# First loads in order of use, x half turned by its load, and B's token sums on VectorE, in a two-block attention kernel on one Trainium2 core

## The chip, the cores and the metric

The kernel runs on one core of a Trainium2 chip. The time is device microseconds of one execution. A profile is one execution taken by the hardware profiler; the other times are of executions without it. Engines: PE is TensorE's matmul, PEld its weight load, DVE is VectorE, ACT ScalarE, POOL GpSimd, SP SyncE, which here issues most loads and stores.

## What is computed

Two blocks on inputs of 2048 tokens and 640 features, 32 heads of 20, results side by side in one output of 2048 x 1280, all bf16:

```python
def _A_ref(x, wqkv, wo):                     # sliding-window attention, window 256
    q, k, v = split_heads(x @ wqkv)
    scores = einsum("bhqd,bhkd->bhqk", q, k) * Dh ** -0.5
    p = softmax(where(0 <= i - j < 256, scores, -1e9))
    return merge_heads(einsum("bhqk,bhkd->bhqd", p, v)) @ wo

def _B_ref(x, wqkv, wo):                     # linear attention
    q, k, v = split_heads(x @ wqkv)
    pq, pk = phi(q), phi(k)                  # phi(t) = t + 1 where t > 0, else exp(t); + 1e-6
    kv = einsum("bhsd,bhse->bhde", pk, v)
    z = einsum("bhsd->bhd", pk)              # sums over the 2048 tokens
    num, den = einsum("bhqd,bhde->bhqe", pq, kv), einsum("bhqd,bhd->bhq", pq, z) + 1e-6
    return merge_heads(num / den) @ wo
```

## The kernel before

The 2048 tokens are worked in four tiles of 512. Every piece of work (a matmul or a group of them, an eviction, a load) is an operation that names its engine and what it depends on. A list written out in the kernel, SEQ, holds all 2089 of them as index x 8 + engine, and they are issued in that order, so it fixes the order of every engine's queue. Each engine runs its queue in order. Operations of A and B are mixed in it.

For block A and a tile: x arrives turned (features on partitions), by a transposing load on SP (`load_x`, L553). The first tile is the exception: four plain loads of 128 tokens each (`x0n`, L1209), which PE turns with an identity (L1242), five transposes each, and DVE evicts. q and k are products with 512 columns (`proj`, L577), v with 320 (`proj_v`, L638). Weights for q and k are first copied into another column order (`cq`, `ck`). Scores go to PSUM in small tiles of the array (`attn`, L708), ACT takes the exponential of 2048 columns at a time (76 times, L724), DVE multiplies the edges by a mask (L736), and PE multiplies by v (L764, "PV", four head groups in a tile). Head groups are written to DRAM and read back in another layout (`a_out`: `oc`, and `osum` with the row sums), a row of reciprocals is made by ACT from a logarithm, DVE multiplies (L860), and `finish_rows` makes 128 output rows (L798: ten matmuls in two halves, two evictions, one store).

For block B: phi(k) of a block of 128 tokens (`b_keys`, L913) stays as `pk` (four tiles in the buffers K0 to K3). `b_sums` (L938) multiplies it with x. `b_z` makes z: 32 matmuls of a column of ones with `pk`, four side by side (L974), so that each of four groups of 32 partitions holds one quarter of the sum; DVE splits it into a high and a low bf16 part (L986, L989) out of PSUM, ten matmuls turn it into a column (L995), and DVE spreads that into `Zc` (L1002). `b_kvwo` multiplies the sums with wv (L1037) and wo (L1055), evicts six rows of 120 (`kvs`), stores them to DRAM and reads them back as `kvwo`. `b_query` makes phi(q) (L1107; ACT L874, DVE L878 and L881), the denominators (`den`, 20 matmuls with 32-column weights, L1125), their reciprocals by ACT, four loads that spread them over the partitions (L1146), the division by DVE (L1171, one product for each 128 tokens), and the output rows (`finish_rows`, L798).

Output rows and `kvs` use four row buffers, O0 to O3: an eviction waits until the store of the row that had the buffer has landed. PSUM gives four banks (F0 to F3) to everything but scores. DVE sets the tile `warm` and a constant `tiny`, PE starts with 20 matmuls of 128 columns on `warm` and four pairs more (`heat`, L1185), and ACT loads its function table first and then issues three of the five loads of wv.

Of the kernel before, what the change touches and what calls it, by code (L numbers as in the profile page):

```python
# [7 lines left out]
P = 128  # L8
ALU = mybir.AluOpType
# [5 lines left out]
PRM = {"sq": "SP", "dens": 4}  # L15
TUNE = {}
SEQ = [
# [372 lines left out]
def build(nc, pools, A_x, A_wqkv, A_wo, B_x, B_wqkv, B_wo, out):  # L390
# [3 lines left out]
    HV = Dh + 1  # L394
    KT = 5
    NT = 16
    NQ = 512
    NTT = 4
    HALF = 320
    WIDE = bool(PRM.get("wide"))  # L400
    SWD = 640 if WIDE else 512
    scale = float(Dh) ** -0.5
    NF = 3 if WIDE else 4
    FB = [f"F{i}" for i in range(NF)]
    pl = Planner(FB + ["S0"] + [f"O{i}" for i in range(PRM.get("nosb", 4))] + ["L0"])

# [385 lines left out]
    def finish_rows(tb, col0, lhs, rhs, key, deps, name):  # L792
# [20 lines left out]
        if SEQ or PRM.get("ast"):  # L813
            st.engs["ACT"] = 430
# [668 lines left out]
```

## Time and profile before

| | us |
|---|---|
| median of 3 runs (lowest, highest) | 250.89 (250.74, 251.39) |
| the profiled execution | 250.49 |
| its span, first to last instruction | 248.8 |
| PE, ACT, DVE busy | 239.9, 200.8, 172.6 |

How to read it: in the chain of waits a piece is a start, a length and the work, followed back from the last instruction to what released it. "x16" counts instructions. In a timeline, brackets hold the idle time of the engine before the piece and what ended it. "F" and "S" are PSUM banks, F for all but scores. Line numbers are those of the kernel before. A few per cent of the matmuls have no record.

### The profile page before, as it was taken

The page shows a single profiled execution, that of the slowest core. Times are in us where ns is not written, and L with a number is a line of the kernel's source. Part 1 is how long each engine was busy: PE and PEld are TensorE (multiplying, and loading weights), DVE is VectorE, ACT ScalarE, POOL GpSimd, SP SyncE. Part 2 cuts the span into 40 slices and gives each one's busy share as a digit, 9 for nine tenths or more (in the row PEclk, how much of TensorE's full clock was granted, in tenths as well). Part 3 has the DMA queues.
Part 4 walks back from the last instruction along what each step waited for, and adds up shares of the span by engine and source line. Part 5 has one row for each costly group of instructions (what it writes and reads, how often), then busy time and mean ns, then how long its engine had stood idle before and what let it go on. Part 6 is the DMA issues. An engine that isn't in the chain of part 4 may idle for free.

```text
span 248.8 us, 9643 instructions
## 1 busy us (share of the span) xinstructions
PE 239.9 (96%) x4167; PEld 144.3 (58%) x4193; DVE 172.6 (69%) x441; ACT 200.8 (81%) x222; POOL 40.4 (16%) x93
## 2 busy tenths in 40 slices
PE   7999999999999999999999999999989999999993
PEld 6644565454655666545566666666555665565671
DVE  2553587778679978886666363369999899949740
ACT  2459898988999999988998788789999987946532
POOL 6003460063002601004078000000000000000000
PEclk9999999999999999999999999999999999999999
DMA  6999226649364759913573768863545472236433
GB/s 216 284 148 243 59 66 148 154 90 166 87 223 111 198 99 213 277 42 72 143 194 75 124 154 258 202 164 105 159 139 151 119 167 84 76 114 186 135 128 111
DMA packets 54216, 36.61 MB, mean 147 GB/s; under 512 B 34249, under 2 KB 52761, under 8 KB 54169
## 3 DMA queue, kind: packets, MB, share of 16 engines
q1 hardware_dynamic: 50537, 31.52, 49.7%
q0 software_dynamic: 2048, 2.63, 5.3%
q10 hardware_dynamic: 1584, 1.80, 2.2%
q8 instruction: 33, 0.54, 1.0%
q14 instruction: 14, 0.11, 0.2%
HBM read 13.90 MB, written 10.26 MB: 97 GB/s over the span
## 4 chain that ended last, share of the span: by engine, by line
PE 87%; ACT 6%; DVE 3%; issue 2%; DMA 1%; ACTq 0%; DVEq 0%
PE F L577 17%; PE F L798 16%; PE S L708 10%; PE F L638 9%; PE F L913 9%; PE F L938 9%; PE F L764 6%; PE F L1107 5%; ACT p L724 4%; DMA out_dram<-osb 1%; PE F L1185 1%; DVE pq L881 1%; PE F L1037 1%; ACT e L874 1%; PE F L1242 1%
## 5 line engine op out<-in xcount | busy, mean ns | idle before, releaser
L724 ACT ACTIVATE p<-S 128x2048 bf16<-128x2048 f32 x76 | 141.1, 1856 | 16.4 <-PE S L708 14.5
L736 DVE TENSOR_TENSOR p<-p,strip 128x256 bf16<-128x256 bf16 (+2 forms) x140 | 49.4, 381 | 21.1 <-ACT p L724 20.5
L874 ACT ACTIVATE e<-F 128x320 bf16<-128x320 f32 (+1 forms) x52 | 25.5, 501 | 8.3 <-PE F L1107 5.8
L638 PE MATMUL F<-wv,xT 128*128 128x320 bf16 x160 | 31.7, 300 | 0.1
L913 PE MATMUL F<-wkB,xT 128*128 128x320 bf16 x160 | 30.7, 299 | 0.2 <-issue 0.2
L798 PE MATMUL F<-woA,oc 128*128 128x320 bf16 x160 | 30.3, 300 | 0.0
L611 POOL DMA_DIRECT2D odd<-st x32 | 18.2, 573 | 69.3 <-ACT st L484 28.8
L577 PE MATMUL F<-xT,wk 128*128 128x512 bf16 x91 | 27.8, 380 | 0.3
L577 PE MATMUL F<-xT,wq 128*128 128x512 bf16 x92 | 26.9, 380 | 0.5 <-issue 0.3
L938 PE MATMUL F<-pk,xtok 128*128 128x320 bf16 x160 | 27.1, 300 | 0.0
L798 PE MATMUL F<-kvwo,pq 128*128 128x320 bf16 x160 | 25.9, 300 | 0.9 <-DVE pq L1171 0.4
L1107 PE MATMUL F<-xT,wqB 128*128 128x512 bf16 x91 | 25.4, 381 | 0.3
L486 DVE CAST ost<-F 128x512 bf16<-128x512 f32 x26 | 17.1, 685 | 10.2 <-PE F L764 10.0
L486 DVE CAST even<-F 128x512 bf16<-128x512 f32 x24 | 16.5, 688 | 8.2 <-PE F L577 7.9
L486 DVE CAST osb<-F 128x320 bf16<-128x320 f32 x33 | 15.5, 486 | 8.6 <-PE F L798 7.9
L608 POOL DMA_DIRECT2D odd<-even x32 | 16.6, 524 | 25.4 <-DVE even L486 23.2
L764 PE MATMUL F<-p,vt 64*32 64x320 bf16 (+4 forms) x720 | 20.5, 253 | 0.0
L638 PEld LDWEIGHTS <-xT 128*128 128x128 bf16 x160 | 15.1, 98 | 9.2 <-issue 1.3
L913 PEld LDWEIGHTS <-xT 128*128 128x128 bf16 x160 | 15.0, 98 | 8.9 <-issue 1.2
L764 PE MATMUL F<-p,sw 64*32 64x320 bf16 (+3 forms) x720 | 19.9, 253 | 0.2 <-DVE kvs L486 0.2
L798 PEld LDWEIGHTS <-pq 128*128 128x128 bf16 x160 | 14.9, 98 | 8.7 <-issue 1.6
L484 ACT CAST osb<-F 128x320 bf16<-128x320 f32 x31 | 12.6, 426 | 8.5 <-PE F L798 6.2
(85 smaller groups left out, 295.8 us busy)
## 6 DMA issues: line engine op xcount, KB each, us to landing
OD<-ost SPq DMA_DIRECT2D x32, 128.0 KB, 2.2
out_dram<-osb SPq DMA_DIRECT2D x24, 160.0 KB, 2.1
oc<-OD SPq DMA_DIRECT2D x4, 640.0 KB, 4.9
xtok<-in_B_x_dram SPq DMA_DIRECT2D x4, 640.0 KB, 4.5
odd<-even POOLq DMA_DIRECT2D x32, 48.0 KB, 2.9
sw<-vt SPq DMA_DIRECT2D x16, 87.0 KB, 3.1
out_dram<-osb ACTq DMA_DIRECT2D x8, 160.0 KB, 2.1
odd<-st POOLq DMA_DIRECT2D x32, 32.0 KB, 3.1
```

What stands on the lines that cost most here:

```text
L486: nc.vector.tensor_copy(out=dst, in_=src)
L577: nc.tensor.matmul(ps[:, a:b], lhsT=w[:, kt, i, :], rhs=xb["t"][:, kt, a:b], start=(kt == 0), stop=(kt == KT - 1))
L638: return lambda ps: nc.tensor.matmul(ps[:], lhsT=xb["t"][:, kt, bb * P : bb * P + P], rhs=rhs_(), start=(kt == 0), stop=(kt == KT - 1))
L708: nc.tensor.matmul(st["s"][64 * i : 64 * i + 64, o0 : o0 + b - a], lhsT=kb["t"][32 * j : 32 * j + Dh, sl, ko : ko + 64], rhs=qb["t"][32 * ...
L724: nc.scalar.activation(out=o_, in_=i_, func=ACT.Exp, scale=scale)
L736: nc.vector.tensor_tensor(out=x, in0=x, in1=mkv[:, None, :].to_broadcast([P, 4, 64 * w]), op=ALU.mult)
L764: nc.tensor.matmul(O[i][32 * j : 32 * j + 32, a:b], lhsT=lhsT, rhs=pb["t"][64 * i : 64 * i + 64, o0 + js * j : o0 + js * j + b - a], start ...
L798: return lambda ps: nc.tensor.matmul(ps[:], lhsT=lhs(c), rhs=rhs(c, hf), start=(c == 0), stop=(c == KT - 1))
L874: nc.scalar.activation(out=eb["t"][:, 0:n], in_=ps[:], func=ACT.Exp)
L913: return lambda ps: nc.tensor.matmul(ps[:], lhsT=xb["t"][:, kt, b * P : (b + 1) * P], rhs=R["wkB"][:, kt, hf * HALF : (hf + 1) * HALF], st ...
L938: return lambda ps: nc.tensor.matmul(ps[:], lhsT=R["xt", tb // 4][:, tb % 4, c * P : (c + 1) * P], rhs=R["pk", tb // 4][:, tb % 4, hf * HA ...
L1107: return lambda ps: nc.tensor.matmul(ps[:], lhsT=R["wqB"][:, kt, :].rearrange("p (f c) -> p c f", c=KT)[:, c, :], rhs=xb["t"][:, kt, :], s ...
```

## The change

- Loads: x's first block goes first on SP and its second first on ACT's queue (before, both on SP); wv follows on both. ACT's table load and its first activation become an operation (`tables`) that stands after ACT's first eviction.
- x's blocks 2 and 3 are turned by two transposing loads of 128 tokens on SP, in place of two plain loads, ten transposes and two evictions. The first tile of x has a block-wise layout, which its q, k and v matmuls read with a stride.
- Token sums: 15 adds on DVE accumulate the 16 blocks of `pk` in fp32 (`zacc`), then the high and low parts come from there in one piece each; the 32 matmuls at L974 go. `Zc` lies in the same buffer as the parts. Before the first denominator, 44 small matmuls are added (`dpad`).
- Warm-up: the operand is a constant of the program, not a tile that DVE sets; 18 matmuls and 16 small ones (`pad`), and two pairs instead of four.
- Row buffers: the buffers K2 and K3 hold output rows too, from when the high and the low part are made (until then a `hold` keeps them).
- PV: in the first tile the pieces are multiplied in their own order; in the others the order is as before.
- SEQ is written anew for the 2097 operations.

```diff
+PRM = {"sq": "SP", "dens": 4, "nwarm": 18, "pad": 4, "nfill": 2, "xT0": 2, "dpad": 11}
 SEQ = [
...
+    XT0 = PRM.get("xT0", 0)
...
+    XO = {"OK2": "K2", "OK3": "K3"} if PRM.get("xo", 1) else {}
+    pl = Planner(FB + ["S0"] + list(XO) + [f"O{i}" for i in range(PRM.get("nosb", 4))] + ["L0"])
+    held = [{} for _ in XO]
+    for g_ in held:
+        pl.op({"SP": 1}, lambda e: None, -(10 ** 8), [], name="hold", slots=(1, "O"), g=g_)
...
-        warm = mk("o", [P, NQ], BF16, "warm", tag="L0")
-        nc.vector.memset(warm[:], 0.0)
-        nc.scalar.preload_act_table_set("natural_log_exp_and_others")
+        warm = nc.const_aps.tensor(1.0, (P, P), BF16)
+        if not XT0:
+            nc.scalar.preload_act_table_set("natural_log_exp_and_others")
...
+                    rhs = xb["t"][:, :, kt, :] if t == 0 and XT0 else xb["t"][:, kt, a:b]
+                    nc.tensor.matmul(ps[:, a:b], lhsT=w[:, kt, i, :], rhs=rhs, start=(kt == 0), stop=(kt == KT - 1))
...
+                turn = [(x[2] - x[1], k, x, pb) for k, (lay, pb, _) in enumerate(ubox) for x in lay]
+                if t:
+                    todo = sorted(turn, key=lambda z: (-z[0], z[1]))
+                    turn = [y for k in range(len(todo) // 2) for y in (todo[k], todo[-1 - k])]
...
+    def row_tile(sb, name):
+        tag = sb["slot"][0]
+        return mk("over", [P, D], BF16, name, tag=XO[tag]) if tag in XO else mk("o", [P, D], BF16, name, tag="osb" + tag)
...
-        def emz(e):
-            ps = [psum(zg, hf, [P, HALF]) for hf in range(2)]
-            for b in range(4):
-                for hf in range(2):
-                    for s in range(4):
-                        nc.tensor.matmul(ps[hf][32 * s : 32 * s + 32, :], lhsT=ones[:], rhs=R["pk", s][:, b, hf * HALF : (hf + 1) * HALF], start=(b == 0), stop=(b == 3), tile_position=(0, 32 * s), skip_group_check=True)
...
+        for k in range(1, NT):
+
+            def add(e, k=k):
+                if "zacc" not in R:
+                    R["zacc"] = mk("const", [P, D], F32, "zacc")
+                blk = lambda i: R["pk", i // 4][:, i % 4, :]
+                nc.vector.tensor_tensor(out=R["zacc"][:], in0=blk(0) if k == 1 else R["zacc"][:], in1=blk(k), op=ALU.add)
+
+            need = pk_ops[2 * k : 2 * k + 2] + (pk_ops[0:2] if k == 1 else [prev])
+            prev = pl.op({"DVE": 730}, add, 4000 + k, need, name=f"zs{k}")
+            g_mm.append(prev)
+
+        def hi(e):
+            hl["t"] = mk("over", [P, 3, D], BF16, "hl", tag="T3")
+            nc.vector.tensor_copy(out=hl["t"][:, 0, :], in_=R["zacc"][:])
+
+        def lo(e):
+            nc.vector.tensor_tensor(out=hl["t"][:, 1, :], in0=R["zacc"][:], in1=hl["t"][:, 0, :], op=ALU.subtract)
+
+        hi_ = pl.op({"DVE": 730}, hi, EVK, [prev, gm], name="z.hi", rel=[(g_, 0) for g_ in held[0:1]])
+        evs = [hi_, pl.op({"DVE": 730}, lo, EVK, [hi_], name="z.lo", rel=[(g_, 0) for g_ in held[1:2]])]
...
+                for i in range(PRM.get("dpad", 0) if t == 0 else 0):
+                    for s_ in range(4):
+                        nc.tensor.matmul(dg["w"][32 * s_ : 32 * s_ + 32, 256:264], lhsT=ones[:], rhs=ones[:, 0:8], start=True, stop=True, tile_position=(0, 32 * s_), skip_group_check=True)
...
+            for i in range(pad):
+                for s_ in range(4):
+                    nc.tensor.matmul(psum(g)[32 * s_ : 32 * s_ + 32, 0:32], lhsT=warm[:, 0:32], rhs=warm[:, 0:32], start=True, stop=True, tile_position=(0, 32 * s_), skip_group_check=True)
...
+        for b, n in ((0, 1), (1, 1), (2, 2))[0 if XT0 == 1 else 2 :]:
+
+            def em(e, b=b, n=n):
+                for i in range(b, b + n):
+                    nc.sync.dma_start_transpose(out=x0_tile()[:, i, :, :], in_=xA[i * P : (i + 1) * P, :])
...
+        def tables(e):
+            nc.scalar.preload_act_table_set("natural_log_exp_and_others")
+            tinyo = mk("const", [P, 1], F32, "tinyo")
+            nc.scalar.activation(out=tinyo[:], in_=tiny[:], func=ACT.Exp)
...
+            x0l.append(dma(em, D_XROW, (-1000, -999, -994, -993)[b], [], name=f"x0n{b}", eng="ACTQ" if XT0 and b else "SP"))
```

More of the change, by code (lines that the diff above doesn't have):

```diff
@@ L637, in mm @@
                         rhs_ = lambda: wv[:, kt, :].rearrange("p (a i n) -> p a i n", a=2, i=2)[:, :, i, :]
+                        if t == 0 and XT0:
+                            return lambda ps: nc.tensor.matmul(ps[:], lhsT=xb["t"][:, bb, kt, :], rhs=rhs_(), start=(kt == 0), stop=(kt == KT - 1))
                         return lambda ps: nc.tensor.matmul(ps[:], lhsT=xb["t"][:, kt, bb * P : bb * P + P], rhs=rhs_(), start=(kt == 0), stop=(kt == KT - 1))
@@ L811, in finish_rows @@
             mms.append(g["mm"])
-        st = dma(lambda e: q_of(e).dma_start(out=out2[tb * P : (tb + 1) * P, col0 : col0 + D], in_=sb["t"][:]), D_STORE, -4000, ends, name="store")
-        if SEQ or PRM.get("ast"):
-            st.engs["ACT"] = 430
+        for a, b, need in [(0, 480, ends[:2]), (480, D, ends[2:])] if last else [(0, D, ends)]:
+            st = dma(lambda e, a=a, b=b: q_of(e).dma_start(out=out2[tb * P : (tb + 1) * P, col0 + a : col0 + b], in_=sb["t"][:, a:b]), (340, 1, int(420 * (b - a) / D), 350), -4000, need, name="store")
+            if SEQ or PRM.get("ast"):
+                st.engs["ACT"] = 430
+            R.setdefault("stores", []).append(st)
         st.rel = [(sb, 0)]
-        R.setdefault("stores", []).append(st)
         return mms
@@ L978, in b_z @@
         hl = {}
         evs = []
-        for hf in range(2):
-            cs = slice(hf * HALF, (hf + 1) * HALF)
-            def hi(e, hf=hf, cs=cs):
-                if "t" not in hl:
-                    hl["t"] = mk("over", [P, 2, D], BF16, "hl", tag="T3")
-                nc.vector.tensor_copy(out=hl["t"][:, 0, cs], in_=psum(zg, hf)[:])
-            def lo(e, hf=hf, cs=cs):
-                nc.vector.tensor_tensor(out=hl["t"][:, 1, cs], in0=psum(zg, hf)[:], in1=hl["t"][:, 0, cs], op=ALU.subtract)
-            a = pl.op({"DVE": dve_ps(HALF)}, hi, EVK, [zo, gm], name="z.hi")
-            evs.append(pl.op({"DVE": dve_ps(HALF)}, lo, EVK, [a], name="z.lo", rel=[(zg, hf)]))
+        prev = None
@@ L1058, in ev2 @@
                         if "t" not in sb:
-                            sb["t"] = mk("o", [P, D], BF16, "kvs", tag="osb" + sb["slot"][0])
+                            sb["t"] = row_tile(sb, "kvs")
                         copy(e, sb["t"][0:120, hf * HALF : (hf + 1) * HALF], ps[:])
@@ L1090, in em @@
             R["wqB"] = mk("w", [P, KT, D], BF16, "wqB", tag="wq")
-            nc.sync.dma_start(out=R["wqB"][:], in_=wBv[:, :, 0:D])
+            for a, b in WSP:
+                nc.sync.dma_start(out=R["wqB"][:, a:b, :], in_=wBv[:, a:b, 0:D])
         R["wq_op"] = dma(em, D_WFULL, key, [R["mm", "q", 3]], name="ld.wqB", earliest=140)
@@ L1184, in em @@
             for i in range(n):
-                nc.tensor.matmul(psum(g)[:, 0:P], lhsT=warm[:, 0:P], rhs=warm[:, 0:P], start=True, stop=True)
-        pl.op({"PE": n * 54}, em, key, [], slots=(1, "F"), g=g, rel=[(g, 0)], name="warm", ni=2 * n)
-    heat(nwarm, -(10 ** 8))
+                nc.tensor.matmul(psum(g)[:, 0:P], lhsT=warm, rhs=warm, start=True, stop=True)
+            for i in range(pad):
+                for s_ in range(4):
+                    nc.tensor.matmul(psum(g)[32 * s_ : 32 * s_ + 32, 0:32], lhsT=warm[:, 0:32], rhs=warm[:, 0:32], start=True, stop=True, tile_position=(0, 32 * s_), skip_group_check=True)
+        pl.op({"PE": n * 54 + pad * 14 + (95 if pad else 0)}, em, key, [], slots=(1, "F"), g=g, rel=[(g, 0)], name="warm", ni=2 * n + 8 * pad)
+    heat(nwarm, -(10 ** 8), PRM.get("pad", 0))
     for i in range(PRM.get("nfill", 4)):
         heat(2, 10 ** 7 + i)
-    pl.free["PE"] = 1450
+    pl.free["PE"] = 1060
     pl.free["SP"] = 1040
-    pl.free["ACTQ"] = 1500
-    pl.free["ACT"] = 2400
+    pl.free["ACTQ"] = 1040 if XT0 else 1500
+    pl.free["ACT"] = 3500 if XT0 else 2400
     pl.net = 2140
@@ L1237, in build @@
             W["c" + which].append(o)
-    for b in range(4):
+    for b in range((4, 0, 2)[XT0]):
         def tr(c, b=b):
@@ L1251, in build @@
         x0n_users.append(g["mm"])
+    x0["ready"] += x0.get("late", [])
     def em_wk(e):
         R["wkB"] = mk("w", [P, KT, D], BF16, "wkB", tag="wB")
-        nc.sync.dma_start(out=R["wkB"][:], in_=wBv[:, :, D : 2 * D])
+        for a, b in WSP:
+            nc.sync.dma_start(out=R["wkB"][:, a:b, :], in_=wBv[:, a:b, D : 2 * D])
     proj(0, "q", [-100, -99, -80, -79, -76], 1)
```

93 lines of the change are left out of this document (48 added, 45 removed), and 187 rows, old and new, of the table SEQ.

## The prediction

> **What bounds the kernel now.** I read the profile's page first, then the table of engine time by stretches, then the chain of waits with its pieces in order of time, and the timelines of single engines where that chain leaves TensorE.
>
> ```profile
> PE 239.9 (96%) x4167; PEld 144.3 (58%) x4193; DVE 172.6 (69%) x441; ACT 200.8 (81%) x222; POOL 40.4 (16%) x93
> ...
> PE 87%; ACT 6%; DVE 3%; issue 2%; DMA 1%; ACTq 0%; DVEq 0%
> ```
>
> TensorE (PE) is busy in 96% of the span and carries 87% of the chain. Work taken off it shortens the kernel one for one, unless ScalarE (ACT) or VectorE (DVE) is full in the same stretch. The stretches say where that is (columns: PE, PEld, DVE, ACT, POOL busy, clock, DMA share, GB/s).
>
> ```profile
> 0.00:10.00 10.00, 8.50 (x75) 7.13 (x76) 3.25 (x9) 2.40 (x5) 3.75 (x23) 1.00 0.78 238
> ...
> 140.00:150.00 10.00, 9.94 (x229) 6.70 (x214) 5.41 (x14) 8.27 (x7) 0.00 (x0) 1.00 0.49 115
> 150.00:160.00 10.00, 10.00 (x229) 6.48 (x228) 2.47 (x6) 7.88 (x7) 0.00 (x0) 1.00 0.94 249
> 160.00:170.00 10.00, 9.93 (x244) 6.26 (x243) 7.25 (x20) 8.38 (x9) 0.00 (x0) 1.00 0.59 157
> 170.00:180.00 10.00, 9.61 (x223) 6.07 (x223) 9.54 (x25) 9.73 (x11) 0.00 (x0) 1.00 0.47 144
> 180.00:190.00 10.00, 9.14 (x139) 5.35 (x140) 9.35 (x24) 9.78 (x12) 0.00 (x0) 1.00 0.46 129
> ...
> 220.00:230.00 10.00, 9.53 (x56) 5.73 (x56) 6.96 (x16) 5.15 (x11) 0.00 (x0) 1.00 0.60 176
> ```
>
> PE is idle 1.50 us in the first ten, 0.39 + 0.86 = 1.25 us between 170 and 190, where DVE and ACT are both nearly full, and 0.47 us between 220 and 230. DVE is half to three quarters free from 140 to 160. That is the map for what follows.
>
> The sum is made against the profiled execution: 250.49 us, of which the span is 248.8. The median of the runs is 250.89, 0.40 above it; I subtract from 250.49 and add the 0.40 at the end.
>
> **The start.** From the chain of waits:
>
> ```profile
> 1.17 0.27 DVE warm L504
> 1.44 0.04 DVE tiny L507
> ...
> 1.50 2.74 PE F L1185 x24
> 4.24 1.20 PE F L1242 x10
> ...
> 5.87 2.26 PE F L638 x16
> 8.13 0.28 PE F L1242 x5
> 8.41 0.27 PE F L638 x2
> 8.68 0.28 PE F L1242 x5
> 8.96 2.04 PE F L638 x15
> ```
>
> and from the timeline of the same stretch:
>
> ```profile
> 1.04 0.88 SPq L1209 DMA_DIRECT2D x0n<-in_A_x_dram  x2
> ...
> 4.70 2.74 SPq L542 DMA_DIRECT2D wkn<-in_A_wqkv_dram  x5
> 4.72 0.45 PEld L1242 LDWEIGHTS <-x0n 128*128 128x128 bf16 x5 [0.22 <-DMA x0n<-in_A_x_dram]
> ```
>
> The warm-up waits for two memsets of DVE until 1.50, while the load queue starts at 1.04. A constant that is there already takes this wait away: up to 0.46 us. The second row block of x then goes out first on ACT's queue instead of second on SP's, 0.88/2 = 0.44 us earlier, which covers the 0.22 us wait; wv's first loads on that queue are behind one issue of 0.44 us, but start 0.46 earlier. ACT's table load moves behind its first eviction, into time in which ACT is 24% busy. The 16 small matmuls (pad) fill time before x has landed. I take 0.40 of between 0 and 0.46: the first group of transposes followed the warm-up without a wait, so that x had landed. [...]
>
> Blocks 2 and 3 of x are turned by their load. That removes two groups of five transposes, 0.28 us each, on a PE that runs without a gap there: 0.56 us. What is late next is the turned load itself:
>
> ```profile
> xT<-in_A_x_dram SPq DMA_TRANSPOSE x3, 7.6
> ...
> x0n<-in_A_x_dram SPq DMA_DIRECT2D x4, 160.0 KB, 3.2
> ```
>
> ```profile
> L553 SPq DMA_TRANSPOSE xT<-in_B_x_dram x8: 2867/3020/4372, 14.4 to 199.0; - x8
> ```
>
> On SP it stands behind three plain issues, so from about 1.04 + 3 x 0.45 = 2.4. A turned load of 512 rows holds the queue 2.87 to 4.37 us; for 128 rows I estimate a quarter, 0.7 to 1.1, twice. Both are out by 4.6 us, where the weights wk, queued behind them, began before at 4.7, so those lose nothing. They land between 6.5 (second out at 3.3, the 3.2 of a plain load of that size) and 10.9 (the 7.6 of a load four times as large). PE wants them after the 20 v matmuls of blocks 0 and 1, 20 x 2.04/15 = 2.7 us after about 5.2, at 7.9. So a stall of 0 to 3.0 us; I take 0, as the plain load's row is the nearest in size, and keep the rest as a rival.
>
> **B's token sums.**
>
> ```profile
> 163.82 1.26 PE F L764 x92
> ...
> 165.88 0.42 PE S L708 x16
> 166.30 1.20 PE F L974 x32
> 167.50 0.34 PE F L1107
> ```
>
> ```profile
> L1002 DVE TENSOR_TENSOR Zc<-blk,zs x1: 826/826/826, 174.5 to 174.5; 128x640 bf16<-128x640 bf16 x1
> ...
> L986 DVE CAST hl<-F x2: 480/486/491, 167.6 to 168.0; 128x320 bf16<-128x320 f32 x2
> L989 DVE TENSOR_TENSOR hl<-F,hl x2: 481/482/484, 168.4 to 171.4; 128x320 bf16<-128x320 f32 x2
> ```
>
> The 32 matmuls at L974 are 1.20 us with PE work directly on both sides: gone in full, -1.20. In their place stand 15 adds on DVE of 128 x 640 and a high and a low part. The nearest row is the product with one fp32 operand over the same 640 elements, 0.83 us: 17 x 0.83 = 14.1, less the four old parts 4 x 0.48 = 1.9, so 12.2 us more on DVE. Its cover is the free time from 140 to 170, 4.6 + 7.5 + 2.75 = 14.8 us. The new order list, read as operations, puts six adds singly or in pairs between masks of A's third tile, seven in a row after the eviction of that tile's third head group, two behind its last masks, and the two parts among the fourth tile's first masks. Behind the seven wait masks whose exponentials ACT has yet to make. I charge nothing; if the cover is gone, each add is 0.83 us.
>
> **The padding before the first denominator.** 44 matmuls of 8 columns with 32-column weights are added on PE. The nearest row is an attention product (L764 above), whose 96 matmuls (92 of them recorded) also have 32-column weights in small tiles: 1.26/96 = 13 ns each, while it streams real columns as well: 44 x 13 ns = 0.58 us at most, 0 at least if PE waits there for its operands anyway. I take +0.30, halfway, because that row's streams hide part of its issue.
>
> **Row buffers and order.** Six buffers instead of four hold output rows, the two new ones only after the low part is made. Where four are too few, the chain shows it:
>
> ```profile
> 240.34 3.43 DMA out_dram<-osb
> ...
> 243.84 0.43 ACT osb L484
> ```
>
> and in the timelines, the first row that of the load queue:
>
> ```profile
> 180.78 4.56 SPq L1073 DMA_DIRECT2D kvd<-kvs  x4
> ...
> 244.32 0.84 PE L798 MATMUL F<-kvwo,pq 128*128 128x320 bf16 x5 [0.40 <-ACT osb L484]
> ```
>
> An eviction waits for a store to land, and the last five matmuls wait for that eviction. PE did other rows meanwhile, so what is won is not 3.43 but the 0.40 of idle PE. The same buffers take the kv rows, whose stores wait at 180.78 in the stretch where DVE and ACT are full; of the 1.25 us idle there I take 0.40, for most of it follows ACT's exponentials, which stay. Between 220 and 230:
>
> ```profile
> 224.75 0.69 DVE pq L881
> 225.44 0.41 DVE pq L1171
> 225.89 0.58 PE F L798 x3
> ```
>
> The rows of B's third tile wait for their division, which DVE does behind two feature maps. In the new list that division stands ahead of two of them and its reciprocals are spread first, so I take 0.40 of the 0.47. PV's pieces keep their number and columns: nothing.
>
> Sum: -0.40 - 0.56 - 1.20 + 0.30 - 0.40 - 0.40 - 0.40 = -3.06, so 247.4 for a profiled execution and 247.8 for the median.
>
> **The rivals.**
>
> *The turned load is late* (landing after 7.9): PE stands up to 3.0 us before the v products of block 3. For it speaks the 7.6 us of the large loads and a DMA share of 0.78 in the first ten us; against it a quarter of the size. Half of it gives 249.3, all of it 250.8; from 2.3 us on the result is no longer faster.
>
> *The clock comes late.* Ten transposes took 1.20 us from 4.24, of which 0.22 was a wait, so 98 ns each; five took 0.28 from 8.13, 56 ns each. The v matmuls from 5.87 run at 2.26/16 = 141 ns, near the later 2.04/15 = 136. So PE runs at about half rate for 5.87 - 1.50 = 4.4 us after its first matmul, although the granted clock of the row 0 to 10 is 1.00. The new warm-up is shorter, 18 x 2.74/24 = 2.1 us, and can leave PE idle before x lands. If that idle starts the 4.4 us anew at about 4.2, the work from 5.2 to 8.6 runs at half rate and 1.7 us are lost: 249.5. [...]
>
> *ScalarE takes the gain back.* From 170 to 190 ACT is 97 to 98% busy. If its exponentials set the time there, what was won before (0.96 + 1.20) and the 0.40 of the kv rows only lengthen that stretch's idle PE; what stays is 0.30 - 0.40 - 0.40 = -0.5, and the result is 250.4. Against it: ACT is only 79 to 84% busy from 140 to 170, so its exponentials can come earlier too.
>
> *VectorE delays the attention* and the kernel becomes slower. The queue is in order: if the seven adds in a row, 7 x 0.83 = 5.8 us, come when masks are ready, the product of that group waits, TensorE runs out of other groups because its banks wait for the same DVE, and ACT waits for free probability buffers. All of it on the path gives 247.8 + 5.8 = 253.6; it eats the gain from 3.1 us on and shows as slower from 3.9. For it speaks that four more additions stand just before the 9.54 of 170 to 180; against it the 2.47 of 150 to 160.
>
> **How the numbers follow.** About 0.3%, 0.75 us, is what a measurement of this kernel tells from no change: faster is under 250.14, slower over 251.64. The forecast has 0.60; late load 0.09, late clock 0.09, ScalarE 0.08, VectorE 0.14. Faster: 0.60 + 0.09 of the clock + 0.06 of the load + 0.02 of ScalarE, where it takes back only a part, = 0.77; within 0.3%: 0.03 + 0.06 = 0.09; slower: 0.14. The forecast's own range goes from 246.4 (all of the 1.25, 0.47 and 0.46 us, no padding cost, and the 0.13 us of idle PE from 140 to 170) to 248.9 (nothing at the start and at the kv rows, 0.28 more for the padding). The range for 8 in 10 reaches up over late clock, half of the late load and ScalarE's case to 250.6 and leaves out VectorE's case, the rest of the load's and a little below.
>
> **What would show it.** Right: warm-up from about 1.1 us, v matmuls from about 5.2 and no transposes after them; no matmul at the sums' line and adds of 0.75 to 0.83 us between 130 and 166; no wait for a store before the last matmuls; fewer than 0.2 us of idle PE after the third tile's reciprocals. Wrong: v matmuls over 0.2 us apart or waiting for xT between 7 and 11; PE idle before the attention product that stood at 163.82, with DVE on the adds; more than 1.25 us of idle PE between 168 and 190.

## The result: slower, and the profile after

The changed kernel took 254.6 us (median of 6 runs, 253.56 to 255.43), the kernel before, measured beside it, 251.14 (250.22 to 251.92): ratio 1.0137, 95% interval 1.011 to 1.0163. The profiled execution took 253.56 us with a span of 252.1 (before 250.49 and 248.8). It is one of the six and the fastest of them, so the two profiles differ by 3.07 us where the medians differ by 3.46. I had forecast 247.8 and a range up to 250.6.

The page of the changed kernel, engine busy times and the chain's shares:

```profile
PE 239.8 (95%) x4180; PEld 143.8 (57%) x4205; DVE 184.9 (73%) x452; ACT 202.1 (80%) x222; POOL 40.5 (16%) x92
...
PE 85%; DVE 5%; ACT 4%; issue 2%; DMA 2%; ACTq 0%; DVEq 0%
```

TensorE is busy as long as before, in a span that is 3.3 us longer, so the loss is time in which it stands. The stretches of the changed kernel:

```profile
0.00:10.00 10.00, 8.15 (x72) 6.09 (x73) 1.47 (x5) 4.17 (x6) 3.72 (x22) 1.00 0.86 235
...
150.00:160.00 10.00, 10.00 (x228) 6.33 (x227) 9.63 (x19) 8.20 (x8) 0.00 (x0) 1.00 0.79 186
160.00:170.00 10.00, 9.95 (x217) 6.20 (x217) 9.02 (x21) 9.62 (x11) 0.00 (x0) 1.00 0.43 135
170.00:180.00 10.00, 9.43 (x225) 6.37 (x225) 9.90 (x24) 9.74 (x10) 0.00 (x0) 1.00 0.58 155
180.00:190.00 10.00, 9.52 (x182) 5.86 (x182) 9.66 (x26) 9.40 (x10) 0.00 (x0) 1.00 0.66 125
190.00:200.00 10.00, 8.47 (x197) 5.27 (x197) 8.82 (x22) 8.95 (x8) 0.00 (x0) 1.00 0.60 143
...
220.00:230.00 10.00, 9.33 (x114) 5.49 (x96) 6.07 (x14) 4.72 (x11) 0.00 (x0) 1.00 0.51 146
```

and the one row of the kernel before that is not shown with the prediction:

```profile
190.00:200.00 10.00, 9.95 (x212) 6.03 (x219) 8.74 (x22) 9.79 (x10) 0.00 (x0) 1.00 0.50 141
```

Where VectorE got its adds, from 150 to 170, TensorE does not stand (0.05 us). It stands 1.53 us from 190 to 200, where it stood 0.05 before; 0.67 from 220 to 230 (0.47 before); and 1.85 in the first ten (1.50 before).

**The start.** Chain of waits, then timelines of TensorE and ScalarE:

```profile
1.97 4.54 DMA wv<-in_A_wqkv_dram
...
6.55 5.03 PE F L646 x32
```

```profile
1.08 2.08 PE L1207 MATMUL F<-const-bfloat16-1.0 128*128 128x128 bf16 x18 [1.08 <-PEq L1516]
3.09 0.30 PE L1210 MATMUL F<-const-bfloat16-1.0 128*32 128x32 bf16 x16
3.93 1.25 PE L1291 MATMUL F<-ident,x0n 128*128 128x128 bf16 x10 [0.54 <-POOL vt L541]
4.97 0.42 PE L1207 MATMUL F<-const-bfloat16-1.0 128*128 128x128 bf16 x2
5.42 0.72 PE L646 MATMUL F<-wv,xT 128*128 128x320 bf16 x2
5.93 0.42 PE L1207 MATMUL F<-const-bfloat16-1.0 128*128 128x128 bf16 x2
6.55 5.03 PE L646 MATMUL F<-wv,xT 128*128 128x320 bf16 x32 [0.20 <-DMA wv<-in_A_wqkv_dram]
```

```profile
2.94 1.28 ACT L491 ACT_TABLE_LOAD   x1 [2.94 <-issue]
4.68 0.69 ACT L491 COPY xT<-F 128x640 bf16<-128x640 bf16 x1 [0.46 <-PE F L1291]
5.39 1.28 ACT L1247 ACT_TABLE_LOAD   x1
```

The warm-up begins at 1.08 as forecast, but is over at 3.2, and x's first block lands at 3.88 (3.35 before). The v matmuls stop after two and go on at 6.55. In the trace each of the first ones holds TensorE for 267 ns, twice the 136 of later ones, until 7.57. The first scores begin at 18.55, 0.44 us later than in the profile before. ScalarE loads a table twice, once at its first copy (L491) and once where the program asks for it (L1247); before, there was one load.

**The stop at 198.** The tile `kvwo` (the transfer and who waited for it), and the load queue ahead of it:

```profile
L1099 SPq DMA_DIRECT2D kvwo<-kvd x2: 485/492/498, 189.0 to 195.0; - x2
...
  PEld L813: 1.6, 1
```

```profile
190.85 0.59 SPq L1088 DMA_DIRECT2D kvd<-kvs  x1
191.49 0.55 SPq L1168 DMA_DIRECT2D recB<-recS  x1
195.04 0.48 SPq L1099 DMA_DIRECT2D kvwo<-kvd  x1
```

The last store of B's small matrix goes out at 190.85, its read-back only at 195.04, and TensorE's rows wait for that until 199.59. The page's waits name a feature map on VectorE beside it (`pq` L897, done at 199.57); it is not the cause, for in run pe24 below the same rows begin at 198.61 and that feature map ends at 199.72. The new order list itself sends the store out 1.9 us later than the old one did (188.95).

**The end.** The last piece of the chain in the kernel before, then the chain of the changed kernel:

```profile
245.20 0.42 ACT osb L484
```

```profile
238.01 8.54 PE F L813 x62
...
246.57 0.49 DVE osb L493
```

The transfers after 245 us by queue (packets, MB, share), first of the changed kernel, then of the one before; q1 has what SP issues, q10 what ScalarE issues, q8 instructions:

```profile
q10 hardware_dynamic: 304, 0.34, 9.0%
q1 hardware_dynamic: 144, 0.16, 4.2%
q8 instruction: 1, 0.02, 0.9%
```

```profile
q1 hardware_dynamic: 288, 0.33, 8.6%
q10 hardware_dynamic: 144, 0.16, 4.2%
```

The last evictions no longer wait for a store: 62 matmuls without a break. But from the last eviction's end, 247.06, to the end of the span there are 5.02 us, where before there were 3.19. What is new there is one transfer on q8: 16 KB of instructions that begin at 246.95, after the last matmul, and take 1.52 us. Of the 432 packets of the last three stores 405 are done by 248.6; the other 27, a sixteenth, come one by one from the end of the fetch on, until 250.1.

### The profile page after: what moved, and what is told of

The parts are those of the page before. It is cut to its first block, busy times and chain, and to the rows that moved or that the text cites. A ratio compares the mean times of both kernels' runs of the same rounds, so it can differ in the third digit from the quotient of the medians.

```text
span 252.1 us, 9681 instructions
## 1 busy us (share of the span) xinstructions
PE 239.8 (95%) x4180; PEld 143.8 (57%) x4205; DVE 184.9 (73%) x452; ACT 202.1 (80%) x222; POOL 40.5 (16%) x92
## 4 chain that ended last, share of the span: by engine, by line
PE 85%; DVE 5%; ACT 4%; issue 2%; DMA 2%; ACTq 0%; DVEq 0%
PE F L813 18%; PE F L584 16%; PE S L717 10%; PE F L954 9%; PE F L929 9%; PE F L774 7%; PE F L647 7%; PE F L1123 6%; ACT p L733 2%; PE F L646 2%; DMA wv<-in_A_wqkv_dram 2%; DVE pq L897 1%; ACT e L890 1%; DVE p L745 1%; PE F L1146 1%
## 5 line engine op out<-in xcount | busy, mean ns | idle before, releaser
L954 PE MATMUL F<-pk,xtok 128*128 128x320 bf16 x160 | 28.3, 300 | 0.0
L584 PE MATMUL F<-xT,wq 128*128 128x512 bf16 x96 | 27.5, 380 | 0.3 <-issue 0.2
L584 PE MATMUL F<-xT,wk 128*128 128x512 bf16 x88 | 26.6, 380 | 0.5 <-ACT e L890 0.2
L647 PE MATMUL F<-wv,xT 128*128 128x320 bf16 x120 | 26.4, 300 | 0.1
L493 DVE CAST even<-F 128x512 bf16<-128x512 f32 x27 | 18.3, 688 | 7.7 <-PE F L584 7.3
L894 DVE TENSOR_SCALAR e<-e 128x320 bf16<-128x320 bf16 (+1 forms) x52 | 13.4, 260 | 9.8 <-ACT e L890 9.1
L774 PE MATMUL F<-p,vt 64*32 64x320 bf16 (+3 forms) x720 | 20.3, 253 | 0.0
L929 PEld LDWEIGHTS <-xT 128*128 128x128 bf16 x160 | 15.1, 98 | 8.9 <-issue 1.5
L491 ACT CAST osb<-F 128x320 bf16<-128x320 f32 x32 | 13.4, 425 | 7.7 <-PE F L813 7.6
```

The lines of the kernel that those rows point to most:

```text
L493: nc.vector.tensor_copy(out=dst, in_=src)
L584: nc.tensor.matmul(ps[:, a:b], lhsT=w[:, kt, i, :], rhs=rhs, start=(kt == 0), stop=(kt == KT - 1))
L647: return lambda ps: nc.tensor.matmul(ps[:], lhsT=xb["t"][:, kt, bb * P : bb * P + P], rhs=rhs_(), start=(kt == 0), stop=(kt == KT - 1))
L774: nc.tensor.matmul(O[i][32 * j : 32 * j + 32, a:b], lhsT=lhsT, rhs=pb["t"][64 * i : 64 * i + 64, o0 + js * j : o0 + js * j + b - a], start ...
L929: return lambda ps: nc.tensor.matmul(ps[:], lhsT=xb["t"][:, kt, b * P : (b + 1) * P], rhs=R["wkB"][:, kt, hf * HALF : (hf + 1) * HALF], st ...
L954: return lambda ps: nc.tensor.matmul(ps[:], lhsT=R["xt", tb // 4][:, tb % 4, c * P : (c + 1) * P], rhs=R["pk", tb // 4][:, tb % 4, hf * HA ...
```

## The experiments

All of them, with the time, that of the kernel before beside it, the ratio with its interval, and from the profiled execution the begin of the first scores and the time from the last eviction to the end of the span (18.11 and 3.19 in the kernel before):

| run | us | before | ratio (95%) | first scores | end |
|---|---|---|---|---|---|
| changed | 254.6 | 251.1 | 1.0137 (1.011, 1.0163) | 18.55 | 5.02 |
| pe24 | 251.67 | 250.8 | 1.0026 (1.0006, 1.0046) | 18.40 | 3.40 |
| kvq | 253.65 | 250.8 | 1.0109 (1.0084, 1.0133) | 18.83 | 5.44 |
| x0plain | 253.87 | 250.8 | 1.0113 (1.0085, 1.0141) | 21.82 | 5.29 |
| zpe | 254.85 | 250.8 | 1.0145 (1.0116, 1.0174) | 18.99 | 5.19 |
| before12 | 252.91 | 251.05 | 1.0058 (1.0036, 1.008) | 18.22 | 5.31 |
| warm26 | 250.77 | 251.05 | 0.997 (0.9945, 0.9995) | 18.66 | 3.37 |
| oldstart | 250.6 | 251.05 | 0.9963 (0.9938, 0.9988) | 18.33 | 3.25 |
| best1 | 250.86 | 251.05 | 0.9988 (0.996, 1.0017) | 17.75 | 3.37 |
| vorder | 249.49 | 250.96 | 0.9942 (0.9923, 0.9962) | 17.64 | 3.37 |
| vorder0 | 251.12 | 250.96 | 1.0003 (0.9985, 1.0021) | 17.58 | 4.59 |
| oldden2 | 250.7 | 250.96 | 0.9996 (0.9979, 1.0014) | 18.54 | 3.22 |
| rows | 250.74 | 250.96 | 0.9995 (0.9973, 1.0017) | 19.04 | 3.53 |
| padmove | 253.67 | 251.1 | 1.0106 (1.0053, 1.016) | 18.17 | 5.38 |
| vkvq | 250.17 | 251.1 | 0.9965 (0.9939, 0.9992) | 17.42 | 3.37 |

The first scores scatter from profile to profile: 18.11 to 19.04 with the old first loads, 18.17 to 18.99 and once 21.82 with the new ones, 17.42 to 18.66 with the new ones and a longer warm-up. A few tenths in that column of a single profile decide nothing.

### The end: pe24, before12

pe24:

```diff
-PRM = {... "dpad": 11}
+PRM = {... "dpad": 8}
```

> The changed kernel with 8 instead of 11 groups of the padding before the first denominator: TensorE's program is 24 instructions shorter, as long as that of the kernel before. Theory A (the 16 KB of TensorE's instructions that are fetched after the last matmul stand in front of the last stores): that fetch goes, the time from the last eviction to the end of the span falls from 5.0 us to 3.2-3.5, and the time from 254.6 to about 253.0. Rival (the last stores are slow because two queues issue them at once): the end stays 5.0 us long and the time falls by at most 0.1 us, for the 12 matmuls.

251.67 us: 12 matmuls of 8 columns fewer, and the ratio goes from 1.0137 to 1.0026, which is 2.8 us, more than the 1.6 expected. The 16 KB after 245 are gone from the transfers, and the end is 3.40 us long:

```profile
q10 hardware_dynamic: 294, 0.33, 8.8%
q1 hardware_dynamic: 144, 0.16, 4.2%
```

The surplus is the stop at 198. It shrank too, to 0.24 us of idle TensorE from 190 to 200, and all behind it came 1.0 us earlier than in the changed kernel:

```profile
190.00:200.00 10.00, 9.76 (x213) 5.85 (x203) 9.22 (x23) 8.61 (x9) 0.00 (x0) 1.00 0.50 133
```

Without these losses the change is still no gain: pe24 is 0.3% above the kernel before.

before12, the same length put into the kernel before, ahead of its first denominator:

```diff
                 ps = psum(dg, 0, [P, P])
+                for i in range(3 if t == 0 else 0):
+                    for s_ in range(4):
+                        nc.tensor.matmul(ps[32 * s_ : 32 * s_ + 32, 0:8], lhsT=ones[:], rhs=ones[:, 0:8], start=True, stop=True, tile_position=(0, 32 * s_), skip_group_check=True)
```

> The kernel before with 12 matmuls of 8 columns added ahead of its first denominator, 24 instructions with their weight loads, so that TensorE's program is as long as that of the changed kernel; they take 12 x 13 ns = 0.16 us. Theory A (behind a certain length of TensorE's program another 16 KB of it are fetched after the last matmul and stand in front of the last stores): a fetch of 16 KB appears after 244, the time from the last eviction to the end grows from 3.2 us to 4.5 or more, the time is 252.2 or more (before 250.8). Rival (that fetch, if it comes, hurts only the new order of the last rows): the time is within 0.4 us of 250.8.

252.91 us. The fetch after 245 appears, and the end grows from 3.19 to 5.31:

```profile
q1 hardware_dynamic: 288, 0.33, 8.9%
q10 hardware_dynamic: 182, 0.19, 4.9%
q8 instruction: 1, 0.02, 1.1%
```

So 0.16 us of work in a kernel with another order of its last rows costs 1.5 us by the ratio, 1.9 by the medians. In all profiles with the long program the end takes 5.0 to 5.4 us, in all with the short one 3.2 to 3.5 (one exception, vorder0, below). The theory holds, the rival falls. Why the fetch comes no run isolates. The queue q8 has 33 such fetches in the profile before and 34 in the changed kernel's, on average some 250 recorded TensorE instructions apart (8360 over 33, 8385 over 34). What pe24 and before12 show is that 24 TensorE instructions fewer take the one after the last matmul away and 24 more bring it. In the changed kernel TensorE's last matmul ends at 246.55, 0.4 us before the fetch begins, so TensorE does not wait for it; what is late beside it are the 27 packets that land from its end on.

### The stop at 198: kvq, padmove

kvq, order list only: the last product of B's small matrix (`kvwo2.1`) ahead of `oa2.1.1`, its eviction and store ahead of the first read-back, the second read-back (`kvr0`) behind the second of the loads that spread reciprocals.

> The changed kernel, only the order list edited: the last product of B's small matrix with wo, its eviction and its store go ahead of the third row block's second half, and the second read-back of the result ahead of two of the loads that spread reciprocals. Theory A (the 1.5 us that TensorE stands at 198 is the late read-back of that matrix): idle TensorE from 190 to 200 falls from 1.53 us to under 0.4, the rows at 199.6 begin at 198.2, the time is about 253.2. Rival (VectorE, filled by the adds, is what is late there): TensorE then waits for the division of pq instead, 0.9 us or more stay idle, and the time is above 254.0.

253.65 us. The read-back goes out at 192.13, idle TensorE from 190 to 200 is 0.17 us, but part of the gain is given back before, at 186, where the moved product makes everything 0.45 us later; the last matmul ends 0.34 us earlier than in the changed kernel, 0.62 if one takes off the later start of this run. The stop is the late read-back, as theory A has it; the time lies between the two forecasts, and its interval overlaps that of the changed kernel.

padmove, the padding before the second denominator instead of the first:

```diff
-                for i in range(PRM.get("dpad", 0) if t == 0 else 0):
+                for i in range(PRM.get("dpad", 0) if t == 1 else 0):
```

> The changed kernel with all 44 padding matmuls ahead of the second denominator instead of the first: the same program length, but from 186 to 204 us TensorE stands 88 instructions earlier in it, so that the fetch of 16 KB that began at 192.22 begins 3 us or more later. Theory A (that fetch shares an engine with the store of B's small matrix, which then lands after 4.2 us instead of 2.1 to 2.5, and the read-back and the rows behind it are late by as much): the second read-back is issued by 193.6 instead of 195.04, idle TensorE from 190 to 200 is under 0.5 us instead of 1.53, the end after the last eviction stays at 5 us, the time is 253.1 to 253.6 (changed kernel 254.6). Rival (the stop at 198 comes from the order of the queues alone, and run pe24 lost it by chance of its start): the stop stays above 1.0 us and the time is 254.2 or more.

253.67 us (251.94 to 254.66). In the profiled execution (252.2), TensorE does not stand at all from 190 to 200, while the end stays 5.38 us long. How long the store took to land, of the changed kernel, of pe24 and of padmove (KB, median us to landing):

```profile
kvd<-kvs SPq DMA_DIRECT2D x1, 100.0 KB, 4.2
```

```profile
kvd<-kvs SPq DMA_DIRECT2D x1, 100.0 KB, 2.5
```

```profile
kvd<-kvs SPq DMA_DIRECT2D x1, 100.0 KB, 2.5
```

The changed kernel's store went out at 190.85 and the fetch of 16 KB began at 192.22, 1.4 us behind it; in pe24 2.3 us behind (190.94, 193.28), in padmove 2.7 (190.22, 192.93). The fetch came later as expected, though by 0.7 us and not by 3. Where it meets the store, the landing and the read-back are late by 1.6 us. The other profiles fit: in the three in which a fetch begins within 1.4 us behind this store (the changed kernel, x0plain at 0.9, zpe at 0.5) it takes 4.2, 3.8 and 3.5 us to land, in the other thirteen, the kernel before among them, 2.0 to 3.2. That a late landing is the usual case of the changed kernel and not only that of the profiled runs stays open: padmove's six runs fall into two groups, 252 to 253 and 254.3 to 254.7.

### Token sums: zpe

```diff
-            prev = pl.op({"DVE": 730}, add, 4000 + k, need, name=f"zs{k}")
+        zo = pl.op({"PE": 1120}, emz, kv("z", key), [pk_ops, gm], mode="z", slots=(2, "F"), g=zg, name="z", cls="Z", ni=64)
```

and the high and low parts by halves out of PSUM, as in the kernel before.

> The changed kernel with the token sums again by 32 matmuls on TensorE and the four parts out of PSUM, in the place where the fourth tile's first masks stand; the 15 adds on VectorE go. Theory A (the adds lie in free time of VectorE and cost nothing): 1.2 us more on TensorE at about 167, everything behind it is later by that, the stop at 198 stays, the time is 255.5 to 255.9. Rival (the adds delay VectorE and so the rows from 170 on): the stop at 198 shrinks by 1 us or more and the time is 254.6 or less.

254.85 us, outside both forecasts and between them; four executions, and their interval overlaps that of the changed kernel. Against the changed kernel, whose order it has, the trace shows the scores that follow the sums 1.62 us later and the next ones 2.0. At the stop 1.4 us come back, since the read-back lands while TensorE is still behind. The last matmul ends 1.94 later, 1.50 without the later start. That is more than the medians show, which differ by 0.25 us: this profile is the slowest of four executions, that of the changed kernel the fastest of six. The 64 instructions more also move the fetch to 0.5 us behind the store, so zpe does not isolate the sums. TensorE, idle for 0.05 us from 150 to 170, does not wait for the adds where they stand:

```profile
L993 DVE TENSOR_TENSOR zacc<-zacc,pk x14: 817/824/827, 148.2 to 165.4; 128x640 f32<-128x640 f32 x14
...
L1001 DVE CAST hl<-zacc x1: 486/486/486, 168.3 to 168.3; 128x640 bf16<-128x640 f32 x1
L1004 DVE TENSOR_TENSOR hl<-zacc,hl x1: 817/817/817, 170.4 to 170.4; 128x640 bf16<-128x640 f32 x1
```

### The start: x0plain, warm26, oldstart

x0plain:

```diff
-                    nc.sync.dma_start_transpose(out=x0_tile()[:, i, :, :], in_=xA[i * P : (i + 1) * P, :])
+                    nc.sync.dma_start(out=x0_tile()[:, i, :, :], in_=xA[i * P : (i + 1) * P, :].rearrange("p (k n) -> p k n", k=KT))
```

> The changed kernel with the two turning loads of x's first tile replaced by plain loads of the same bytes to the same place, so half of that tile is not turned (the rest is computed as before). Theory A (the turning loads share the 16 DMA engines with wv's loads and hold wv back): wv is there by 5.7, the v matmuls run on from 5.4 without the stop until 6.55, the first scores come about 1.0 us earlier (17.6 instead of 18.6), the time is about 253.5. Rival (the second table load and the eviction of x's first block by ScalarE make the start late): v still stops until 6.5 and the time stays within 0.3 us of 254.6.

253.87 us; the time is near the theory's, with an interval that overlaps that of the changed kernel, but in the profile the theory falls: v stopped until 7.49. Of the 16 parts in which wv's third slice lands, 15 were there by 6.35, the last at 7.44; in the changed kernel 15 by 6.15 and the last at 6.51. So wv is late without turning loads too. This execution, with 256.74 the longest of its kernel, shows another cause:

```profile
7.49 5.76 PE L646 MATMUL F<-wv,xT 128*128 128x320 bf16 x21 [1.11 <-DMA wv<-in_A_wqkv_dram]
```

5.76/21 = 274 ns a matmul: TensorE went on at half rate until 13.3 us, and the first scores came 3.3 us later than in the changed kernel.

warm26 (with the short program):

```diff
-PRM = {..., "nwarm": 18, "pad": 4, "nfill": 2, "xT0": 2, "dpad": 11}
+PRM = {..., "nwarm": 26, "pad": 0, "nfill": 2, "xT0": 2, "dpad": 8}
```

> The changed kernel with the short program of run pe24 and a warm-up of 26 matmuls of 128 columns without the 16 small ones, so that TensorE is busy from 1.1 to about 3.9, when x's first blocks land. Theory B (the idle 0.7 us between warm-up and transposes makes the clock come late: v at 267 ns for 320 columns until 7.5 to 8.4 us, and to 13.3 in one run): v runs at 136 ns from 5.8 at the latest, the first scores come at 17.4 to 17.9 instead of 18.4, the time is 250.6 to 251.0 (pe24 251.67). Rival (the start is set by the last part of wv, which lands at 6.2 to 6.5, and TensorE waits for it): the first scores come after 18.1 and the time is above 251.3.

250.77 us, 0.6% below pe24 by the ratios. Busy from 1.08, TensorE has its full rate at about 4.6, and v runs at 4.51/32 = 141 ns although it waited a microsecond for wv:

```profile
7.19 4.51 PE L646 MATMUL F<-wv,xT 128*128 128x320 bf16 x32 [1.00 <-DMA wv<-in_A_wqkv_dram]
```

Each was right in part: the full rate comes early and the time is the theory's, but behind the clock stands wv, and the profiled run's first scores came no earlier than in pe24. In all six profiles with the short warm-up the full rate comes at 7.2 us or later, in all five with 26 matmuls by 4.8. What it is worth in time is less sure: warm26 also has 16 TensorE instructions fewer than pe24, and 24 fewer moved the fetches in pe24. From the first matmul at 1.08 to the full rate it is about 3.5 us here; in the changed kernel, with its gap at 3.2, it is 3.6 us from the transposes at 3.93 to 7.57; in x0plain 5.8 us from the end of its gap at 7.49 to 13.3.

oldstart: the changed kernel with the short program and everything up to the first exponential in the order of the kernel before, `"nwarm": 20, "pad": 0, "nfill": 4, "xT0": 0, "dpad": 8`, and the four plain loads.

> The changed kernel with the short program of run pe24 and the first 18 us of the kernel before in their old order: four plain loads of x, 20 transposes, the function table first; only the warm-up keeps its operand, the constant. My forecast of the change (the new start saves 0.40 for its loads and 0.56 for the transposes, of which the constant's share stays here): the time is 0.6 to 0.9 above pe24, 252.3 or more. Theory B (the new start loses by its late clock and by late wv more than the transposes take): first scores at 17.7 to 18.1 instead of 18.4, the time is 251.0 to 251.4.

250.6 us; my forecast for it, 252.3, falls. The new start with its ten transposes fewer was worth less than the old one, by 0.6% of the ratio, with programs of the same length. The two profiled executions (pe24 250.91, oldstart 250.71) do not show where it lies.

### Division, order of v, padding, row buffers: best1, vorder, vorder0, oldden2, rows, vkvq

best1: warm26, kvq's moves, and the division `nrmB2.2` on VectorE ahead of `qB3.0`'s feature map.

> Run warm26 with three moves in the order list: the third row block of B's small matrix earlier as in run kvq, and in front of the last tile's first feature map the first division of the third tile. Theory A and B together (short program, early clock, no late read-back, and 0.6 us of idle TensorE at 225 that is the division waiting behind a feature map on VectorE): under 0.3 us idle from 190 to 200, under 0.2 from 220 to 230, the time is 249.6 to 250.2. Rival (the wait at 225 is the reciprocals' way over the spreading loads, not the order on VectorE): the idle time from 220 to 230 stays above 0.4 us and the time is 250.3 or more.

250.86 us, with or without the one execution of twelve at 253.85. Idle TensorE from 220 to 230 is 0.00, so the wait was the order on VectorE, and the rival's cause falls; from 190 to 200 it is 0.35. But the time is the rival's: against warm26 nothing is won.

vorder: warm26, the division, and the v products that need only wv's first two slices ahead of the first that needs the third.

In the names the digits are tile, block of 128 tokens and half, and behind # stands the slice:

```diff
 order of v: 0.0.1#0, 0.0.1#1, warm#2,
-  0.0.1#2, 0.1.0#0, 0.1.0#1, 0.0.0#0, 0.0.0#1, ...
+  0.1.0#0, 0.1.0#1, 0.0.0#0, 0.0.0#1, 0.1.1#0, 0.1.1#1, 0.0.1#2, ...
```

> Run warm26 with two moves in the order list: the v products of the first two feature slices for all four groups stand ahead of the first product that needs wv's third slice, as in the kernel before; and the first division of the third tile ahead of the last tile's first feature map. Theory B (the start is late by the clock, cured by the longer warm-up, and by a TensorE queue that asks for the third slice of wv at its third product): no wait above 0.3 us between 5.5 and 10, first scores at 17.3 to 17.7 (pe24 18.4), under 0.2 us idle from 220 to 230, the time is 249.3 to 249.8. Rival (wv comes late whatever the order, by the transfers that share the engines): TensorE waits for wv for 0.5 us or more and the time is above 250.2.

249.49 us (249.28 to 249.92): faster than both kernels, 0.6% below the one before. Against warm26, which has neither move, it is 0.3% by the ratios, with intervals that overlap. Six products fill part of the time until wv lands, and the wait left is 0.44 us, more than the 0.3 expected:

```profile
5.46 0.98 PE L657 MATMUL F<-wv,xT 128*128 128x320 bf16 x6
6.88 3.79 PE L657 MATMUL F<-wv,xT 128*128 128x320 bf16 x26 [0.44 <-DMA wv<-in_A_wqkv_dram]
```

vorder0: vorder with `"dpad": 0`.

> Run vorder without the padding before the first denominator: 32 small matmuls and 64 instructions fewer. Theory (the padding stands on the path, 0.41 us for 44 of them): 0.3 us less than vorder. Rival (it only fills time in which TensorE waits there, or the fetches of instructions, now 64 instructions later, meet another transfer that is waited for): no gain, or 0.5 us or more above vorder.

251.12 us, 1.6 us worse for less work: the second rival. TensorE's last matmul ends 1.0 us earlier (243.54 against 244.55), and the span 0.2 later. The fetch of the running program, at 242.3 in vorder, now begins at 243.85, beside the last stores, the last of which goes out at 244.10:

```profile
239.88 3.68 PE F L824 x27
...
243.58 0.49 DVE osb L504
```

Its end takes 4.59 us, against 3.37 in vorder. The two profiles differ by 0.2 us only, since that of vorder0 (250.14) is one of the fastest of its twelve executions and that of vorder (249.92) the slowest of its six; they show the later end, not all of the 1.6. The padding itself stands on the path, with 0.41 us in the chain of the changed kernel:

```profile
186.24 0.41 PE F L1142 x44
```

oldden2: oldstart with the division moved.

> Run oldstart with the first division of the third tile ahead of the last tile's first feature map on VectorE. Theory (that wait of 0.62 us is the order on VectorE): under 0.2 us idle from 220 to 230 and the time is 249.9 to 250.1 (oldstart 250.6). Rival (another wait takes its place before the end): 250.4 or more.

250.7 us, no gain: the 0.62 us left the stretch 220 to 230 and came back in the next. VectorE's queue stops at a product of A that waits for its read-back, and the feature map behind it is what the last denominator needs (timelines of VectorE and TensorE):

```profile
230.49 0.49 DVE L888 TENSOR_TENSOR oc<-oc,recA 128x640 bf16<-128x640 bf16 x1 [1.18 <-DMA oc<-OD]
```

```profile
231.97 0.48 PE L1158 MATMUL F<-pq,hl 128*32 128x128 bf16 x20 [0.61 <-DVE pq L909]
```

rows: the kernel before with `OK2` and `OK3` as two more row buffers, its order list unchanged.

> The kernel before with the two more row buffers alone, its own order list, TensorE's program as long as before. My forecast of this part (0.40 us of idle TensorE before the last five matmuls, which wait for a store, and up to 0.40 at the kv rows): no wait for a store at the end, the time is 250.2 to 250.7 (before 251.05). Rival (the wait is only moved, to the evictions or to the queues that issue the stores): within 0.2 us of 251.05.

250.74 us against 250.96, not told apart from no change. The 57 last matmuls run without a break, so the wait for a store is gone; from the last denominator to the last matmul the trace is 0.56 us shorter, and the end 0.34 longer (3.53).

vkvq: vorder with kvq's moves.

> Run vorder with the third row block of B's small matrix and its store earlier, as in run kvq, so that no fetch of instructions meets that store. Theory A: the 0.8 us that TensorE stands from 190 to 200 in vorder shrink to 0.4 or less, the time is 249.0 to 249.3. Rival (the earlier product takes VectorE's time from the feature maps, which cost 0.45 us at 187 in run best1): the time is 249.5 or more.

250.17 us, 0.2% above vorder by the ratios with intervals that overlap. The idle time from 190 to 200 shrank to 0.39, as theory A had it, but the time is the rival's: no gain.

## Why the prediction was wrong

The sum had -3.06; the spans differ by +3.28, 6.3 us away. Its steps, in its own order:

- **The start, -0.40 and -0.56: +0.44 in the two profiles, 1.4 us off.** The size rests on two profiles of a start that scatters; that the gain did not come is also what oldstart says, 0.6% below pe24. The constant did take the wait away. But x's block lands at 3.88 and not at 3.35, 0.53 us later. Whether the second block beside it or wv's loads delay it, no run isolates. The larger part is the rival of the late clock, with the idle time that it names: the shorter warm-up leaves 0.7 us of idle TensorE, and the full rate comes at 7.57 instead of 5.93, 3.6 us behind the idle time where I had 4.4. The sum had it at nothing; as a rival I had it at 1.7 us and gave it 0.09. It is also the one sign of being wrong that came true: v products 0.27 us apart between 7 and 7.6. The rival of the late turned load did not happen: the two blocks landed at 7.57 and 8.19, and TensorE, itself late by then, waited for neither, though they held the queue 2.82 us and not twice 0.7 to 1.1.
- **The token sums, -1.20: the mechanism held, the gain in time is not shown.** The 1.20 us of matmuls are gone, the adds took 0.82 us as said, the high part 0.49, and TensorE waited for none of them. zpe, which takes this back, ends 1.5 us later in its profile, but its median is only 0.25 us longer. The rival of VectorE, to which I gave the largest chance of a slower kernel, did not happen in the profile; that the kernel became slower, which only this rival forecast, came about another way.
- **The padding, +0.30: 0.41,** 9 ns for each of the 44 matmuls. That the streams of the attention product hide part of its issue, for which I took half of 0.58, no run shows.
- **Row buffers, -0.40: the wait went, the time hardly;** rows shows -0.22 with an interval around nothing. **kv rows, -0.40:** idle TensorE from 170 to 190 fell from 1.25 to 1.05, and to 0.80 in pe24.
- **The division, -0.40: nothing won, 0.67 us idle against 0.47, 0.60 off.** I had read in the new list that it stands ahead of two feature maps; one still stood before it, and that one was waiting for ScalarE:

```profile
225.34 0.69 DVE pq L897
226.03 0.41 DVE pq L1193
```

- **What the sum did not have: two fetches of instructions.** The step that failed most is the base of the sum, "I subtract from 250.49": only TensorE's work and waits were changed there, and what follows the last eviction and the landing of the kv store stayed as they were, at nothing and without a reason. The end grew by 1.83 us. The stop at 198 adds 1.48. pe24 shows both together, 2.8 us of the 3.4 by which the kernel is slower, taken away by 24 instructions that do next to no work. The rest of the miss is in the terms above: pe24, too, gains nothing where 3.06 us were forecast.

1.40 + 1.83 + 1.48 + 0.60 for the division + 0.20 for the kv rows + 0.11 for the padding make 5.6 of the 6.3 between these two profiles, with the token sums and the row buffers taken as won; the rest I have not assigned. The kernel did come out slower, but by none of the paths to which the prediction gave that chance.

## What to carry to other kernels

Count the instructions, not only the time: 24 TensorE instructions fewer moved the fetch behind the kv store from 192.22 to 193.28 here and took the one at 246.95 away, and a fetch beside a store that someone waits for cost 1.6 us at the kv store and 1.8 at the end. Before judging a change in a tuned kernel, look at what moves after the last matmul and try the same change with a few dozen instructions more or less. In this kernel the warm-up had to last until its first real operand lands (full rate by 4.8 us, else at 7.2 or later), and the best version asks for the weights in the order in which they land.

## What I had not expected of the hardware

- One transfer of 16 KB of instructions takes 0.9 to 1.9 us in these traces, and a 100 KB store issued up to 1.4 us ahead of one lands after 3.5 to 4.2 us instead of 2.0 to 3.2; the end behind the last eviction grows from 3.2 to 3.5 us to 4.6 to 5.4.
- The granted clock reads 1.00 in a row in which TensorE runs at half its rate (267 against 136 ns for 320 columns): the half rate of the first microseconds is to be read from the matmuls.
- The last of the 16 parts of one load can land 1.1 us behind the other 15 (7.44 against 6.35), and the waiting TensorE goes on at 7.49, behind that one part.
- With a copy on ScalarE ahead of the program's table load there are two loads of 1.28 us, at 2.94 and 5.39; with the program's load first, at 1.04, there is one.
